# An attention kernel whose last block is rearranged: second half normalised without a cast in between, its guard on GpSimd, the last store issued by ScalarE, closing waits on five engines

## The chip, the cores and the metric

The kernel runs on one core of a Trainium2 chip. The metric is device microseconds of one execution, as the median of several runs; lower is better. One more execution is recorded by the hardware profiler, and its trace gives the rows that are quoted here. Engines: PE is TensorE's matmuls and PEld its weight loads, DVE is VectorE, ACT is ScalarE, POOL is GpSimd, SP is SyncE; a name with a q behind it (SPq, ACTq, POOLq) is that engine's sequencer, which issues DMAs, waits and branches.

## The reference: what is computed

Two attention blocks on different inputs, their outputs side by side. S is 2048 positions, D 640 channels, 32 heads of 20 channels, all in bf16.

```python
qkv = (x @ wqkv).reshape(B, S, 3, H, Dh)          # both blocks
# A: softmax attention
scores = jnp.einsum("bhqd,bhkd->bhqk", q, k) * (Dh ** -0.5)
o = jnp.einsum("bhqk,bhkd->bhqd", softmax(scores), v)
a = o.reshape(B, S, D) @ wo
# B: linear attention
phi = lambda t: jnp.where(t > 0, t + 1, jnp.exp(t)) + 1e-6
kv = jnp.einsum("bhsd,bhse->bhde", phi(k), v); z = phi(k).sum(s)
o = (phi(q) @ kv) / (phi(q) @ z + 1e-6)
b = o.reshape(B, S, D) @ wo
return jnp.concatenate([a, b], axis=-1)
```

## The kernel before

Block A does nearly all the work. It is cut into 32 blocks: 4 chunks of 512 queries times 8 groups of 4 heads. For each block and each of 16 tiles of 128 keys, PE makes the scores of the four heads, and their exponential is taken: by ScalarE for most tiles (L1976), by VectorE and GpSimd for 4 or 5 tiles of each block (L1829 turns a score into an integer that is the bits of a bf16 power of two, L2047 adds constants to four of these at once with a 64-bit add on GpSimd). PE multiplies the result with V into one PSUM bank, with a column of ones in V so that the softmax's denominator comes along. Block B's steps fill the gaps.

At the end of a block, `norm` (L2053 and on) has VectorE transpose the bank, take the reciprocal of the denominators into f_Rt, multiply into f_T and transpose back into f_OTn, from where a DMA spreads it for the output projection. The last block does this in two halves of 256 queries (`half`, L2073), so that the projection of the first half can start early. That last projection is cut into seven pieces (`CLOSE`, L795): for each the planner opens a PSUM bank with the groups that are done, and `step_close` adds the last group, has the engine that CLOSE names cast the piece into f_PT (L1420), and when the five columns of 128 of a tile are complete, issues its store (L1409). Tile 0 and 1 belong to the first half, tile 2 and 3 to the second.

The kernel skips the usual subtraction of the row maximum, so a guard (`check`, L2155) looks at the reciprocals: two compares against 1e-30 and 1e28 into a scratch (printed as f_xT), a reduction with minimum into f_sm (L2168), one small matmul over the partitions and two small steps (L2180, L2182) that leave a flag of 0 or 1. The reciprocals of the earlier blocks are looked at once before the end; those left over are looked at behind the last half. At the very end every engine reads the flag (L2429) and branches (L2432): to the end, or to a general version that computes block A anew (not run for these inputs). The end is `finish` (L198): waits for each of 24 DMA semaphores, two to an instruction.

The order of instructions on each engine is made when the program is built: a planner (`run`, `try_pe`, `try_q`) plays through estimated times, and each engine's queue gives, of the steps that are ready, the one of lowest `prio`. What it decides is then fixed; on the chip each engine runs its list in order, and waits at semaphores.

At the start, GpSimd loads the library that holds the 64-bit add (L1097) and makes the identity matrix f_id (MEMSET L1099, AFFINE_SELECT L1100). PE first runs 16 matmuls on zeros (f_zt), then transposes the first four tiles of x with f_id (L1126), then makes the first projections of Q and K.

Of the kernel before, what the change touches and what calls it, by code (L numbers as in the profile page):

```python
# [42 lines left out]
class _Sched:  # L43
# [152 lines left out]
                    eng.h.wait_ge(self.sems[key], 16 * cnt)  # L196

    def finish(self):  # L198
        sp = self.eng["sp"]
        for key, cnt, _ in self.dma_slots:  # L200
            if cnt > 0:
                sp.h.wait_ge(self.sems[key], 16 * cnt)


def _split_units(nunits):
# [519 lines left out]


class _Op:
    __slots__ = ("eng", "fn", "reads", "writes", "occ", "lat", "prio", "seq", "after", "ok", "dma")

    def __init__(self, eng, fn, reads, writes, occ, lat, prio, seq, after=None, ok=None):  # L730
        self.eng = eng
        self.fn = fn
        self.reads = reads
        self.writes = writes
        self.occ = occ
        self.lat = lat
        self.prio = prio
        self.seq = seq
        self.after = after
        self.ok = ok  # L740
        self.dma = eng == "sp"


def _c_dve(n):
    return 1.042 * n + 68
# [35 lines left out]
class _Fast:  # L781
# [10 lines left out]
    QO = "xVKVQKVQKV"  # L792
    HINT = {mybir.EngineType.PE: 3, mybir.EngineType.Activation: 9, mybir.EngineType.DVE: 6,
            mybir.EngineType.Pool: 13, mybir.EngineType.SP: 15}
    CLOSE = (("dve", 0, ((0, 0, 512),)), ("act", 0, ((1, 0, 512),)), ("act", 0, ((0, 512, 640), (1, 512, 640))),  # L795
             ("dve", 1, ((2, 0, 320),)), ("act", 1, ((2, 320, 640),)),
             ("dve", 1, ((3, 0, 320),)), ("act", 1, ((3, 320, 640),)))
    NS = 7
# [189 lines left out]
    def emit(self, op):  # L988
        e = op.eng
        t = max(self.free[e], self.est(e, op.reads, op.writes))  # L990
        if op.dma and e == "pool":
            s = max(t + 1450.0, self.dfree)
            self.dfree = s + 2900.0
            op.lat += s - t - 1450.0 + (2000.0 if t < 32000.0 else 0.0)
        if op.dma:
            self.sch.dma(e, op.fn, reads=op.reads, writes=op.writes)
        else:
            self.sch.op(e, op.fn, reads=op.reads, writes=op.writes)
        self.free[e] = t + op.occ
        self.mark(e, op.reads, op.writes, t + op.lat)  # L1000
        if op.after is not None:
            op.after()
# [390 lines left out]
    def step_close(self, qc, p):  # L1393
        eng, half, parts = self.CLOSE[p]
        flat = self.PT[:].rearrange("p t n -> p (t n)")
        w = parts[0][2] - parts[0][1]
        sl = [flat[:, 1024 * t + c0:1024 * t + c1] for t, c0, c1 in parts]
        if len(parts) == 2:
            t, c0, c1 = parts[0]
            sl = flat[:, 1024 * t:1024 * (t + 2)].rearrange("p (t n) -> p t n", n=1024)[:, :, c0:c1]  # L1400
        else:
            sl = sl[0]

        def fin(b):
            self.abank.append(b)
            for t, c0, c1 in parts:
                self.clw[t] = self.clw.get(t, 0) + c1 - c0
                if self.clw[t] == D_MODEL:
                    self.push("sp", lambda e, t=t: e.dma_start(  # L1409
                        self.out[512 * qc + 128 * t:512 * qc + 128 * (t + 1), 0:D_MODEL],  # L1410
                        flat[:, 1024 * t:1024 * t + D_MODEL]),
                        tuple(("cl", q) for q, c in enumerate(self.CLOSE) if any(y[0] == t for y in c[2])),
                        (("out", "a", t),), 500, prio=-1, lat=3000)

        def post(b):
            src = self.ps[:, b, 0:w * len(parts)]
            if len(parts) == 2:
                src = src.rearrange("p (t n) -> p t n", n=w)
            n = w * len(parts)
            self.push(eng, (lambda e: e.copy(sl, src)) if eng == "act" else (lambda e: e.tensor_copy(sl, src)),  # L1420
                      (("ps", b),), (("cl", p),), _c_act(n) if eng == "act" else _c_dve(n), prio=0,
                      after=lambda: fin(b))
        st = _Step(lambda b: self.out_mms(b, qc, parts, (6,)), post, needs=(("open", p),), key=("out", p))
        st.bank = p
        return st
# [624 lines left out]
    def norm(self, n):  # L2050
# [22 lines left out]
        def half(h):  # L2073
            c = slice(256 * h, 256 * (h + 1))
            bl = slice(8 * h, 8 * (h + 1))
            res = (("OTn", o), ("OTn", o, h))
            nxt = (lambda: (self.close(0), half(1))) if h == 0 else (lambda: self.normed(n))
            self.push("dve", lambda e: e.transpose(ps[:, b, c], ps[:, b, c]), (), (("ps", b),), 330, prio=-1,
                      ok=lambda: ("OTn", n - 1) in self.done, after=lambda: self.push(
                          "dve", lambda e: e.reciprocal(R[:, bl], Tv[:, bl, 0]), (("ps", b),), (("Rt", n),), 120,  # L2080
                          prio=-1, after=lambda: self.push(
                              "dve", lambda e: e.tensor_tensor(
                                  T2v[:, bl, 1:21], Tv[:, bl, 1:21],
                                  R[:, bl].unsqueeze(2).broadcast_to([128, 8, D_HEAD]), op=ALU.mult),
                              (("ps", b), ("Rt", n)), ("T2",), _c_dve(160), prio=-1,
                              after=lambda: (freed() if h else None, self.push(
                                  "dve", lambda e: e.transpose(self.OTn[:, o, c], self.T2[:, c]), ("T2",), res,
                                  330, prio=-1, after=nxt,
                                  ok=lambda: self.opv[n] is None or ("OTs", self.opv[n]) in self.done)))))
        if n == self.NN - 1:  # L2090
            half(0)
            return
        self.push("dve", lambda e: e.transpose(ps[:, b, :], ps[:, b, :]), (), (("ps", b),), 630, prio=-1,  # L2093
# [13 lines left out]
    def normed(self, n):  # L2107
# [39 lines left out]
                    ("dd", "bfin"))))  # L2147
        if g == N_GRP - 1 and last:
            self.close(1)
            assert self.chk >= 0  # L2150
            self.check(self.chk + 1, n)
        if last and self.chk < 0 and ("Q", self.NN - 1) in self.done and not self.qa:
            self.sch.barrier(("dve", "pool"), tuple(x for k in range(self.NQC) for x in self.xt(k)))
            self.chk = n
# [2 lines left out]
    def check(self, n0, n1):  # L2157
# [3 lines left out]
        w = b - a  # L2161
        G = self.gt[:, k, 0:2 * w]
        rd = tuple(("Rt", n) for n in range(n0, n1 + 1))
        self.push("dve", lambda e: e.tensor_scalar(G[:, 0:w], R, 1e-30, None, op0=ALU.is_ge), rd, (("G", k),),
                  _c_dve(w), prio=3, after=lambda: self.push(
                      "dve", lambda e: e.tensor_scalar(G[:, w:2 * w], R, 1e28, None, op0=ALU.is_le),
                      rd + (("G", k),), (("G", k),), _c_dve(w), prio=3, after=lambda: self.push(
                          "dve", lambda e: e.tensor_reduce(self.gm[:, k:k + 1], G, axis=AX.X, op=ALU.min),  # L2168
                          (("G", k),), (("gm", k),), _c_dve(2 * w), prio=3,
                          after=lambda: (self.done.add(("gm", k)), self.prio.append(self.step_flag()) if k == 1 else None))))  # L2170

    def step_flag(self):
# [331 lines left out]
```

## Time and profile before

| what | value |
|---|---|
| median of 3 runs | 718.08 us (718.06 to 720.66) |
| the profiled execution | 718.23 us |
| its span, first to last instruction | 716.5 us |
| TensorE clock granted | 0.998 |
| busy: PE, ACT, DVE, POOL | 98%, 97%, 86%, 46% of the span |

The span is what the rows of the profile count in; 1.73 us lie around it. Times in a row are microseconds from the start of the span. In a timeline a row gives start, length, engine, line, operation and tiles, then how many instructions it groups, and in brackets the idle time before it with what ended that. A row of one line's instructions gives their durations as least, median and largest in ns, and the starts of the first and the last.

### The profile page before, as it was taken

Reading aid. Unit: us, or ns where it says so; the run is one execution under the profiler, and the core shown is the slowest. Engines: PE = TensorE matmul, PEld = TensorE weight load, DVE = VectorE, ACT = ScalarE, POOL = GpSimd, SP = SyncE. Lnnn points to the kernel's source line nnn. Section 1 sums busy time; section 2 is a strip of 40 time slices with the busy share of each in tenths; the row PEclk is TensorE's granted clock in tenths of the full one; section 3 lists DMA queues with packets and bytes.
Section 4 is the critical chain, followed back from the end, with each engine's and each line's share of the span. In section 5 each row is a group of like instructions: output and inputs, shape, how many; then the busy total and the mean of one; then the engine's idle time right before and its main releaser. Section 6 shows DMA issues by size and latency. Waiting matters only on the chain.

```text
span 716.5 us, 25681 instructions
## 1 busy us (share of the span) xinstructions
PE 701.2 (98%) x11235; PEld 243.1 (34%) x11235; DVE 614.0 (86%) x1107; ACT 691.9 (97%) x772; POOL 331.1 (46%) x331
## 2 busy tenths in 40 slices
PE   8999999999899999999999999899999999999998
PEld 5433333333223332332432343233332333333323
DVE  6989878888888899989899987899898888998993
ACT  4789999999999999999999999999999999999996
POOL 7643344544445454445534355423454444443552
PEclk9999999999999999999999999999999999999999
DMA  9401010102330011010000112201021100010001
GB/s 264 108 19 36 16 25 14 38 11 74 84 62 11 17 49 43 3 37 21 13 12 9 38 37 86 47 21 28 15 49 31 48 18 8 27 28 7 20 17 48
DMA packets 46554, 27.59 MB, mean 39 GB/s; under 512 B 30842, under 2 KB 45882, under 8 KB 46442
## 3 DMA queue, kind: packets, MB, share of 16 engines
q1 hardware_dynamic: 43818, 23.98, 13.7%
q10 hardware_dynamic: 2624, 1.97, 1.0%
q8 instruction: 88, 1.44, 0.8%
q14 instruction: 24, 0.20, 0.1%
HBM read 8.40 MB, written 5.24 MB: 19 GB/s over the span
## 4 chain that ended last, share of the span: by engine, by line
PE 57%; ACT 39%; DVE 3%; DMA 1%; issue 0%; SPq 0%; ACTq 0%; DVEq 0%
PE ps L166 56%; ACT f_PT L1976 37%; DVE f_Sr L1829 2%; ACT f_ar L1468 2%; DMA f_PT<-in_A_x_dram 1%; DVE ps L2093 0%; PE ps L1047 0%; DVE f_ar L1274 0%; DVE f_st L1027 0%; PE ps L1126 0%; DVE f_PT L1420 0%; DVE f_Qr L1295 0%; DVE f_KT L1295 0%; DVE f_sq L1258 0%; SPq L1067 0%
## 5 line engine op out<-in xcount | busy, mean ns | idle before, releaser
L1976 ACT ACTIVATE f_PT<-ps 128x1024 bf16<-128x1024 f32 x724 | 675.2, 1088 | 13.0 <-PE ps L166 12.2
L2047 POOL INT64_ADD f_Sr<-f_Sr x300 | 307.7, 1041 | 366.2 <-PE ps L166 320.4
L1829 DVE TENSOR_SCALAR f_Sr<-ps 128x512 int16<-128x512 f32 x600 | 401.4, 683 | 65.4 <-PE ps L166 60.1
L166 PE MATMUL ps<-f_Qr,f_KT 32*128 32x512 bf16 x2048 | 285.0, 385 | 8.7 <-ACT f_PT L1976 7.2
L166 PEld LDWEIGHTS ps<-f_Qr,f_KT 32*128 32x128 bf16 x2048 | 71.6, 91 | 256.1 <-ACT f_PT L1976 228.6
L166 PE MATMUL ps<-f_ar 128*32 128x512 bf16 (+6 forms) x3024 | 144.6, 295 | 0.8 <-DVE f_Sr L1829 0.4
L166 PE MATMUL ps<-f_PT,f_V 128*21 128x512 bf16 x1448 | 135.1, 383 | 0.1
L166 PE MATMUL ps<-f_Sr,f_V 128*21 128x512 bf16 x1200 | 108.4, 384 | 0.0
L166 PEld LDWEIGHTS ps<-f_ar 128*32 128x32 bf16 x3024 | 55.8, 96 | 59.2 <-issue 37.2
L166 PE MATMUL ps<-f_Sr,f_Vp 128*21 128x512 bf16 x600 | 57.6, 382 | 0.0
L166 PEld LDWEIGHTS ps<-f_PT,f_V 128*21 128x21 bf16 x1448 | 34.3, 90 | 46.9 <-issue 38.7
L166 PEld LDWEIGHTS ps<-f_Sr,f_V 128*21 128x21 bf16 x1200 | 26.9, 90 | 34.1 <-issue 25.2
L166 PE MATMUL ps<-f_ar,f_xT 128*32 128x160 bf16 x1280 | 33.9, 234 | 0.5 <-DVE f_Sr L1829 0.2
L166 PE MATMUL ps<-f_wo,f_OTd 128*32 128x512 bf16 (+5 forms) x608 | 30.4, 302 | 0.0
L166 PE MATMUL ps<-f_xT,f_ar 128*32 128x512 bf16 x400 | 29.7, 382 | 0.0
L1470 DVE TENSOR_SCALAR f_ar<-f_ar 128x512 bf16<-128x512 bf16 x40 | 23.7, 592 | 4.0 <-ACT f_ar L1468 2.7
L1472 DVE SCALAR_TENSOR_TENSOR f_ar<-ps,f_ar 128x512 bf16<-128x512 f32 x40 | 26.9, 673 | 0.2
L166 PEld LDWEIGHTS ps<-f_ar,f_xT 128*32 128x32 bf16 x1280 | 22.4, 96 | 13.6 <-issue 8.6
L1468 ACT ACTIVATE f_ar<-ps 128x512 bf16<-128x512 f32 x40 | 26.6, 664 | 0.0
L1027 DVE CAST f_st<-ps 128x512 bf16<-128x512 f32 x35 | 23.9, 682 | 2.9 <-PE ps L166 2.6
L166 PE MATMUL ps<-f_xT,f_wq 128*32 128x512 bf16 x320 | 24.1, 383 | 0.0
L2093 DVE STREAM_TRANSPOSE ps<-ps 128x512 f32<-128x512 f32 x31 | 22.5, 725 | 1.8 <-PE ps L166 1.7
(76 smaller groups left out, 279.2 us busy)
## 6 DMA issues: line engine op xcount, KB each, us to landing
out_dram<-f_st SPq DMA_DIRECT2D x35, 128.0 KB
f_ar<-in_B_wqkv_dram SPq DMA_DIRECT2D x15, 160.0 KB
f_OTd<-f_OTn SPq DMA_DIRECT2D x105, 20.0 KB
f_Qr<-f_sq SPq DMA_DIRECT2D x88, 20.0 KB
f_KT<-f_ar SPq DMA_DIRECT2D x22, 80.0 KB
f_ar<-in_A_wqkv_dram SPq DMA_DIRECT2D x1, 800.0 KB
f_ar<-in_A_wqkv_dram ACTq DMA_DIRECT2D x1, 800.0 KB
f_wq<-in_A_wqkv_dram ACTq DMA_DIRECT2D x1, 800.0 KB
```

The source lines that it names most:

```text
L166: lambda e: e.matmul(out, lhsT, rhs, start=start, stop=stop, tile_position=tp, skip_group_check=sgc),
L1027: (lambda e: e.tensor_copy(sl, ps[:, b, 0:w])), (("ps", b),), (res,),
L1468: self.push("act", lambda e: e.activation(r1, src, AF.Exp), (("ps", b),), (rk,), _c_act(n), prio=0, ok=ok, after=lambda: self.push("dve", ...
L1470: "dve", lambda e: e.tensor_scalar(r1, r1, 1.0, 1e-6, op0=ALU.min, op1=ALU.add), (rk,), (rk,),
L1472: "dve", lambda e: e.scalar_tensor_tensor(dst, src, 0.0, r1, op0=ALU.max, op1=ALU.add),
L1829: post = lambda: self.push("dve", lambda e: e.tensor_scalar(self.Sr[:, s, i, :], self.ps[:, b, :], 0.0, 32639.0 - self.PH[-1], op0=ALU.max ...
L1976: return _Op("act", lambda e: e.activation(self.PT[:, s0:s0 + n, :], ps[:, b0:b0 + n, :], AF.Exp, scale=math.log(2.0) / 128.0, bias=self.l ...
L2047: self.q["pool"].append(_Op("pool", lambda e: e.int64_add(v, v, inc), res, res, self.C64, self.C64 + 150, 0, self.seq, after))
L2093: self.push("dve", lambda e: e.transpose(ps[:, b, :], ps[:, b, :]), (), (("ps", b),), 630, prio=-1, ok=lambda: n == 0 or ("OTn", n - 1) in ...
```

## The change

Only the last block and the end are touched.

- `finish` deals the 24 waits in turn to PE, ScalarE, GpSimd, VectorE and SyncE.
- In `CLOSE`, the cast of tile 0's first 512 columns goes from VectorE to ScalarE, and that of the last 128 columns of tiles 0 and 1 from ScalarE to VectorE.
- In `half`, transpose, reciprocal and multiply are one item for the planner (`parts`), so that no other step of VectorE comes between them.
- The second `check` is pushed when the last half is multiplied, its two compares run on GpSimd, and its reduction has the prio -0.5 in place of 3.
- The store of tile 3 is issued by ScalarE.

```diff
     def finish(self):
-        sp = self.eng["sp"]
+        engs = [self.eng[n] for n in ("pe", "act", "pool", "dve", "sp") if n in self.eng]
+        k = 0
         for key, cnt, _ in self.dma_slots:
             if cnt > 0:
-                sp.h.wait_ge(self.sems[key], 16 * cnt)
+                engs[k % len(engs)].h.wait_ge(self.sems[key], 16 * cnt)
+                k += 1
...
-    CLOSE = (("dve", 0, ((0, 0, 512),)), ("act", 0, ((1, 0, 512),)), ("act", 0, ((0, 512, 640), (1, 512, 640))),
+    CLOSE = (("act", 0, ((0, 0, 512),)), ("act", 0, ((1, 0, 512),)), ("dve", 0, ((0, 512, 640), (1, 512, 640))),
              ("dve", 1, ((2, 0, 320),)), ("act", 1, ((2, 320, 640),)),
              ("dve", 1, ((3, 0, 320),)), ("act", 1, ((3, 320, 640),)))
...
-            self.sch.op(e, op.fn, reads=op.reads, writes=op.writes)
+            for fn, rd, wr in op.parts or ((op.fn, op.reads, op.writes),):
+                self.sch.op(e, fn, reads=rd, writes=wr)
...
                 if self.clw[t] == D_MODEL:
-                    self.push("sp", lambda e, t=t: e.dma_start(
+                    q = "act" if t == 3 else "sp"
+                    self.push(q, lambda e, t=t: e.dma_start(
                         self.out[512 * qc + 128 * t:512 * qc + 128 * (t + 1), 0:D_MODEL],
...
+            self.push("dve", None, (), (("ps", b), ("Rt", n), "T2"), 980, prio=-1,
+                      ok=lambda: ("OTn", n - 1) in self.done,
+                      after=lambda: ((freed(), self.check(self.chk + 1, n)) if h else None, self.push(
+                          "dve", lambda e: e.transpose(self.OTn[:, o, c], self.T2[:, c]), ("T2",), res, 440, prio=-1,
+                          after=nxt, ok=lambda: self.opv[n] is None or ("OTs", self.opv[n]) in self.done)))
+            self.q["dve"][-1].parts = (
+                (lambda e: e.transpose(ps[:, b, c], ps[:, b, c]), (), (("ps", b),)),
+                (lambda e: e.reciprocal(R[:, bl], Tv[:, bl, 0]), (("ps", b),), (("Rt", n),)),
+                (lambda e: e.tensor_tensor(T2v[:, bl, 1:21], Tv[:, bl, 1:21],
+                                           R[:, bl].unsqueeze(2).broadcast_to([128, 8, D_HEAD]), op=ALU.mult),
+                 (("ps", b), ("Rt", n)), ("T2",)))
...
             self.close(1)
-            assert self.chk >= 0
-            self.check(self.chk + 1, n)
...
-        self.push("dve", lambda e: e.tensor_scalar(G[:, 0:w], R, 1e-30, None, op0=ALU.is_ge), rd, (("G", k),),
-                  _c_dve(w), prio=3, after=lambda: self.push(
-                      "dve", lambda e: e.tensor_scalar(G[:, w:2 * w], R, 1e28, None, op0=ALU.is_le),
-                      rd + (("G", k),), (("G", k),), _c_dve(w), prio=3, after=lambda: self.push(
+        eng, p, cost = ("pool", 0, 240) if k else ("dve", 3, _c_dve(w))
+        self.push(eng, lambda e: e.tensor_scalar(G[:, 0:w], R, 1e-30, None, op0=ALU.is_ge), rd, (("G", k),),
+                  cost, prio=p, after=lambda: self.push(
+                      eng, lambda e: e.tensor_scalar(G[:, w:2 * w], R, 1e28, None, op0=ALU.is_le),
+                      rd + (("G", k),), (("G", k),), cost, prio=p, after=lambda: self.push(
                           "dve", lambda e: e.tensor_reduce(self.gm[:, k:k + 1], G, axis=AX.X, op=ALU.min),
-                          (("G", k),), (("gm", k),), _c_dve(2 * w), prio=3,
+                          (("G", k),), (("gm", k),), _c_dve(2 * w), prio=-0.5 if k else 3,
```

What the planner makes of this on VectorE, from the reciprocal of the second half to the branch. ps is PSUM, f_Rt the reciprocals, f_T the normalised half, f_PT the casts for the stores, f_sm the guard's minimum; a row's brackets name the engines whose semaphores it waits for. Before:

```order
L2080 RECIPROCAL f_Rt<-ps 128x8 [waits f_sem_dve]
L1420 CAST f_PT<-ps 128x512 [waits f_sem_pe]
L2082 TENSOR_TENSOR f_T<-ps,f_Rt 128x8x20 [waits f_sem_dve]
L2087 STREAM_TRANSPOSE f_OTn<-f_T 128x256 [waits f_sem_dve]
L2164 TENSOR_SCALAR f_xT<-f_Rt 128x64
L2166 TENSOR_SCALAR f_xT<-f_Rt 128x64 [waits f_sem_dve]
L1420 CAST f_PT<-ps 128x320 [waits f_sem_pe] x2
L2168 TENSOR_REDUCE f_sm<-f_xT 128x1 [waits f_sem_dve]
L2180 TENSOR_REDUCE f_g<-ps 1x1 [waits f_sem_pe]
```

And now:

```order
L2091 RECIPROCAL f_Rt<-ps 128x8 [waits f_sem_dve]
L2092 TENSOR_TENSOR f_T<-ps,f_Rt 128x8x20 [waits f_sem_dve]
L1426 CAST f_PT<-ps 128x2x128 [waits f_sem_pe]
L2087 STREAM_TRANSPOSE f_OTn<-f_T 128x256 [waits f_sem_dve]
L2173 TENSOR_REDUCE f_sm<-f_xT 128x1 [waits f_sem_pool]
L1426 CAST f_PT<-ps 128x320 [waits f_sem_pe] x2
L2185 TENSOR_REDUCE f_g<-ps 1x1 [waits f_sem_pe]
```

The 512-wide cast is gone from between reciprocal and multiply, a cast of 2x128 stands behind the multiply, the two compares have left, and the reduction stands ahead of the two last casts, with a wait for GpSimd.

GpSimd, from its 64-bit adds on (printed ISA f_Sr). What stands behind the branch (COMPARE_AND_BRANCH) belongs to the general version. An ISA row without tiles is an instruction that names a library of GpSimd; one more stands at the program's start, for L1097. Before:

```order
L2054 BRANCH_PREFETCH_HINT
L2047 ISA f_Sr<-f_Sr 128x1024 x114
L2429 TENSOR_LOAD f_flag
L2432 COMPARE_AND_BRANCH
L303 MEMSET a_wkp 128x5120
L304 MEMSET a_wqp 128x5120
L314 ISA
L314 IOTA a_ident_i 128x128
```

And now:

```order
L2060 BRANCH_PREFETCH_HINT
L2053 ISA f_Sr<-f_Sr 128x1024 x114
L2169 ISA
L2169 TENSOR_SCALAR f_xT<-f_Rt 128x64
L2171 TENSOR_SCALAR f_xT<-f_Rt 128x64
L2434 TENSOR_LOAD f_flag
L2437 COMPARE_AND_BRANCH
L305 MEMSET a_wkp 128x5120
L306 MEMSET a_wqp 128x5120
L316 IOTA a_ident_i 128x128
```

The two compares have come, and the bare ISA row, which stood in the general version ahead of IOTA, now stands ahead of the first compare, in the part that is always run. The code does not name it; the build puts it in, ahead of an instruction that the add's library does not hold.

ScalarE, from its exponentials on. Before:

```order
L1976 ACTIVATE f_PT<-ps 128x1024 [waits f_sem_pe] x60
L1420 CAST f_PT<-ps 128x512 [waits f_sem_pe]
L1420 CAST f_PT<-ps 128x2x128 [waits f_sem_pe]
L1420 CAST f_PT<-ps 128x320 [waits f_sem_pe] x2
L2429 TENSOR_LOAD f_flag [waits f_sem_dve]
```

And now:

```order
L1982 ACTIVATE f_PT<-ps 128x1024 [waits f_sem_pe] x60
L1426 CAST f_PT<-ps 128x512 [waits f_sem_pe] x2
L1426 CAST f_PT<-ps 128x320 [waits f_sem_pe] x2
L1414 DMA out_dram<-f_PT 128x640 [waits f_sem_act,f_sem_dve]
L2434 TENSOR_LOAD f_flag [waits f_sem_dve]
```

The 2x128 cast has become a second 512-wide one, and the last store stands behind the casts and waits for VectorE's part of them.

More of the change, by code (lines that the diff above doesn't have):

```diff
@@ L727 @@
 class _Op:
-    __slots__ = ("eng", "fn", "reads", "writes", "occ", "lat", "prio", "seq", "after", "ok", "dma")
+    __slots__ = ("eng", "fn", "reads", "writes", "occ", "lat", "prio", "seq", "after", "ok", "dma", "parts")
     def __init__(self, eng, fn, reads, writes, occ, lat, prio, seq, after=None, ok=None):
@@ L741, in __init__ @@
         self.dma = eng == "sp"
+        self.parts = ()
 def _c_dve(n):
@@ L1413, in fin @@
                         (("out", "a", t),), 500, prio=-1, lat=3000)
+                    self.q[q][-1].dma = True
         def post(b):
@@ L2077, in half @@
             nxt = (lambda: (self.close(0), half(1))) if h == 0 else (lambda: self.normed(n))
[L2078 to L2089, printed above, removed]
+            self.push("dve", None, (), (("ps", b), ("Rt", n), "T2"), 980, prio=-1,
[9 more added lines that the diff above has]
+                 (("ps", b), ("Rt", n)), ("T2",)))
         if n == self.NN - 1:
+            assert self.chk >= 0
             half(0)
```

## The prediction

> **What bounds the kernel now.** The page comes first: its first part gives each engine's share of the span.
>
> ```profile
> span 716.5 us, 25681 instructions
> PE 701.2 (98%) x11235; PEld 243.1 (34%) x11235; DVE 614.0 (86%) x1107; ACT 691.9 (97%) x772; POOL 331.1 (46%) x331
> ```
>
> TensorE is busy for 98% and ScalarE for 97%. So whatever holds TensorE up at the start moves the whole program to the right, and whatever holds up the last stores is added at the end; between the two there is nothing to win, and the change touches only the end. The busy times by stretch say how early that begins (columns: stretch, its length, then busy time and count of PE, PEld, DVE, ACT, POOL, then clock, DMA share, GB/s):
>
> ```profile
> 0.00:5.00 5.00, 3.94 (x22) 2.75 (x23) 0.71 (x7) 1.49 (x2) 1.20 (x8) 1.00 0.60 161
> 5.00:10.00 5.00, 4.77 (x65) 3.33 (x63) 2.73 (x7) 1.39 (x2) 3.67 (x5) 1.00 1.11 338
> 10.00:15.00 5.00, 4.41 (x98) 2.48 (x94) 4.85 (x10) 2.93 (x4) 5.00 (x5) 1.00 1.26 276
> 15.00:20.00 5.00, 4.99 (x154) 2.74 (x142) 4.59 (x9) 3.93 (x5) 5.00 (x4) 1.00 1.15 263
> ```
>
> From 15 us on PE has no hole (4.99 of 5.00). A delay in the first 10 us that every matmul inherits is therefore paid in full.
>
> Then the last 10 us, from the timelines of VectorE, ScalarE, GpSimd and SyncE (start, length, instruction, count):
>
> ```profile
> 706.59 1.05 POOL L2047 INT64_ADD f_Sr<-f_Sr  x1 [2.48 <-PE ps L166]
> ...
> 710.76 0.21 DVE L2080 RECIPROCAL f_Rt<-ps 128x8 f32<-128x8 f32 x1
> 710.98 0.69 DVE L1420 CAST f_PT<-ps 128x512 bf16<-128x512 f32 x1
> 711.59 0.32 DVE L2082 TENSOR_TENSOR f_T<-ps,f_Rt 128x160 bf16<-128x160 f32 x1
> 711.94 0.45 DVE L2087 STREAM_TRANSPOSE f_OTn<-f_T 128x256 bf16<-128x256 bf16 x1
> 712.31 0.15 DVE L2164 TENSOR_SCALAR f_xT<-f_Rt 128x64 f32<-128x64 f32 x1
> 712.49 0.20 DVE L2166 TENSOR_SCALAR f_xT<-f_Rt 128x64 f32<-128x64 f32 x1
> 712.81 0.89 DVE L1420 CAST f_PT<-ps 128x320 bf16<-128x320 f32 x2
> 713.62 0.28 DVE L2168 TENSOR_REDUCE f_sm<-f_xT 128x1 f32<-128x128 f32 x1
> 714.17 0.15 DVE L2180 TENSOR_REDUCE f_g<-ps 1x1 f32<-1x2 f32 x1 [0.28 <-PE ps L166]
> 714.35 0.14 DVE L2182 TENSOR_SCALAR f_flag<-f_g 1x1 int32<-1x1 f32 x1
> ...
> 711.19 0.86 ACT L1420 CAST f_PT<-ps 128x512 bf16<-128x512 f32 x2 [2.88 <-PE ps L166]
> 712.95 0.75 ACT L1420 CAST f_PT<-ps 128x320 bf16<-128x320 f32 x2 [0.89 <-PE ps L166]
> ...
> 712.13 2.12 SPq L1409 DMA_DIRECT2D out_dram<-f_PT  x4
> ```
>
> VectorE works without a hole from the reciprocal of the second half to the reduction of the guard at 713.90, then the flag follows at 714.49. The lines that use the flag and the closing waits:
>
> ```profile
> L2429 SPq TENSOR_LOAD <-f_flag x1: 738/738/738, 714.5 to 714.5; - x1
> ...
> L202 SPq EVENT_SEMAPHORE  x12: 28/28/28, 715.5 to 716.2; - x12
> ```
>
> Every engine reads the flag (0.74 us) and branches; then SyncE alone runs 12 wait instructions, 0.06 us apart (0.76 us by their starts and the end of the last, 715.52 to 716.28), none of them held up. DMA traffic of the window 712.0 to 716.5 (40 slices of 0.1125 us):
>
> ```profile
> DMA  0000000029998999930069997999810000000022
> ```
>
> The last store's traffic ends in the thirtieth slice, by 715.4. Its issue ended at 712.13 + 2.12 = 714.25, so it needs 1.15 us more.
>
> **The change part by part.** The kernel's own time is the profiled execution's: 718.23 us, 1.73 more than its span, and 0.15 over the median 718.08; sums are made on 718.23. By "what a measurement of this kernel can tell from no change" I take 0.5%, 3.6 us.
>
> *Second half without a cast in between.* The 0.69 us CAST that stood between reciprocal and multiply goes to ScalarE, the multiply follows at 711.0 and a CAST of 2x128 comes behind it; by the 320-wide one (0.89 for two) I price it at 0.4. The transpose to f_OTn then ends at about 712.07 instead of 712.39: 0.3 us won ahead of the last matmuls and casts. ScalarE's extra 512-wide cast lies in its hole of 2.88 us before 711.19 or behind it, ended by 711.9: free.
>
> *Guard on GpSimd.* VectorE loses 0.15 + 0.20 us of compares, which in before lie while PE makes the last matmuls (CAST waits until 712.81), so nothing is won there. But the reduction moves ahead of the two last CASTs of VectorE and waits for GpSimd. Behind that wait stand the two CASTs, behind them the store that ScalarE now issues, and the flag.
>
> *Last store on ScalarE.* Its issue no longer queues behind the third on SyncE; it follows the last CAST, as now. Between 0 and 0.4 us (one issue, a quarter of the 2.12 us of four, less its wait) won; I take 0, since the fourth issue began only as the CAST had ended.
>
> *Multiply, reciprocal and transpose as one planned item* fixes their order and adds no instruction; PE's last small matmul now also waits for a bank that ScalarE frees, by 713.70 as now, before the reduction is there: nothing.
>
> *Closing waits over five engines.* 24 waits become 4 or 5 per engine: 2 or 3 of the 12 instructions instead of 12, 0.06 us each: 0.5 us less, down to the landing of the last store, which lies about where the waits begin now. The cover is that landing; without a later landing the end is 715.6 to 715.7.
>
> Were this all, the end would come 0.9 us earlier: 717.3.
>
> *The library switch.* The rows of the instruction order show one more instruction than the diff: ahead of GpSimd's first compare stands a bare ISA row. Such a row stands once more on the executed path, at L1097, where the code loads the GpSimd library that holds the 64-bit add. What the profile makes of that one:
>
> ```profile
> L1097 POOLq MODIFY_POOL_CONFIG  x2: 11/11/11, 0.9 to 0.9; - x2
> ...
> 0.96 0.20 POOL L1099 MEMSET f_id<- 128x128 bf16 x1 [0.45 <-POOLq L2489]
> 1.24 0.29 POOL L1100 TENSOR_SCALAR_AFFINE_SELECT f_id<-f_id 128x128 bf16<-128x128 bf16 x1
> ```
>
> Two instructions of 11 ns, and GpSimd is at work 0.03 us later. That is one bound: a switch costs nothing. But in before the execution that went ahead left the same library in place (its last GpSimd work is the 64-bit add), so I read these rows as a switch to what is there already, which says nothing on a real one. In the changed kernel each execution ends with the other library, so it would pay twice: for that one at the end, and for the add's library at its start. No row shows code being loaded. The nearest are transfers from HBM, cold, in the same first microseconds:
>
> ```profile
> 0.80 1.10 ACTq L1071 DMA_DIRECT2D f_ar<-in_A_wqkv_dram  x2
> ...
> 4.97 0.38 POOL L1143 COPY f_wqp<-f_ar 128x240 bf16<-128x240 bf16 x1 [2.97 <-DMA f_ar<-in_A_wqkv_dram]
> 6.62 0.39 POOL L1143 COPY f_ar<-f_ar 128x240 bf16<-128x240 bf16 x1 [1.27 <-DMA f_ar<-in_A_wqkv_dram]
> ```
>
> The first 160 KB were usable 4.2 us after their issue, the second 5.3 us after theirs (issued halfway, at about 1.3). A real switch is one such transfer (4.2) at least, and two of them one after the other (9.5) at most, since it is two instructions; I take the middle, 6.8 us.
>
> At the start the identity matrix f_id is made behind the switch, and PE's transposes wait for it:
>
> ```profile
> 4.45 1.27 PE L1126 MATMUL ps<-f_id,f_PT 128*128 128x128 bf16 x10
> 5.95 1.24 PE L1126 MATMUL ps<-f_id,f_PT 128*128 128x128 bf16 x10 [0.23 <-DMA f_PT<-in_A_x_dram]
> 6.99 1.07 PE L166 MATMUL ps<-f_zt 128*128 128x256 bf16 x8
> 8.02 1.26 PE L166 MATMUL ps<-f_xT,f_wqp 128*32 128x512 bf16 x20
> ```
>
> Now f_id is ready at 1.53, 0.6 behind the switch, and waits 2.9 us for the first x tiles: that is the cover. With 6.8 us it is ready at 0.93 + 6.8 + 0.6 = 8.33; the first ten transposes run 8.4 to 9.66, the second ten start there instead of at 5.95: 3.7 us late. The projections and all else behind follow. So the start costs 3.7 (1.1 with 4.2 us, 6.4 with 9.5).
>
> At the end the ISA row waits for nothing, so it starts behind the last 64-bit add, at 707.64. The compares need the reciprocal of 710.97: 3.3 us of cover. With 6.8 us GpSimd is ready at 714.44. Two compares: by the AFFINE_SELECT row 0.29 each with 0.08 between, as between that row and the MEMSET before it (bounds 0.15, VectorE's own, and 0.39, the COPY): 715.10. Reduction 715.15 to 715.43, CASTs (0.89) to 716.34, ScalarE's issue (0.38) to 716.77, traffic 1.15 to 717.9, then 0.3 for a last wait and the closing (716.28 to 716.5 now): 718.25 against 716.5, that is 1.75 late. The flag comes out level: its two small steps (0.32) behind the CASTs and 1.03 from its end to the first closing wait, as now, give 717.7, and three waits 717.9. (With 4.2 us the compares end at 712.5, the reduction fits ahead of the CASTs almost free, and the end comes 0.8 early; with 9.5 it is 4.4 late.)
>
> Sum: 718.23 + 3.7 + 1.75 = 723.7. Ends: 718.23 + 1.1 - 0.8 = 718.5 and 718.23 + 6.4 + 4.4 = 729.0.
>
> [...]
>
> **The rivals.**
>
> *The switch is free.* For it: the only switch in this trace is (11 ns). Against: that one changed nothing. Then the start stands as it is and the end comes 0.9 earlier: 717.3, no change that can be told. It decides for any load under 2.9 us at the start (the cover of f_id) and 3.3 at the end. Chance 0.20.
>
> *The load begins only with the first call.* The instruction itself takes 11 ns and returns, so the load may wait until a compare asks for it, at 711.0, and the 3.3 us of cover are gone. The end is then 3.4 later than forecast (717.8 instead of 714.44): 727.1. At the start nothing differs, as the AFFINE_SELECT calls at once. Chance 0.15. [...]
>
> *One end only.* If something between two executions puts the add's library back, the start stays and only the end pays: 720.0. If the end's load is covered and the start pays: 718.23 + 3.7 - 0.9 = 721.0. Nothing in one trace tells. Chance 0.12.
>
> *More than that.* PE idles from the end of its first warm-up matmuls at 4.65 to 8.4. Those ran slowly at first:
>
> ```profile
> 1.06 3.59 PE L166 MATMUL ps<-f_zt 128*128 128x256 bf16 x16 [1.06 <-DVE f_sm L1104]
> ```
>
> 16 in 3.59 us is 0.22 each, against 0.13 for the eight of 6.99. If PE falls back to that pace for as long again, 1.5 us come on top, 725.2 for the forecast; with a load of over 9.5 us the time goes past 728. Chance of over 728: 0.08.
>
> **How the numbers follow.** The forecast itself, both ends paid and the load begun by the instruction, has 0.45; its own range is 721.9 to 726.0. Below 721.7 (0.5% over the median) lie the free switch, the single ends and a tenth of the forecast: 0.20 + 0.12 + 0.04, of which 0.02 I leave for a gain of over 3.6 us that no row supports. Slower by over 0.5%: 0.41 + 0.15 + 0.08 and a little of the single ends, 0.65. The range must reach the free switch, since without it 0.28 would be left out: 717.2 to 727.6, which leaves out the longest loads alone.
>
> **What would show each step.** In the changed profile: MODIFY_POOL_CONFIG a second time, at the guard's line, after 707; a hole on GpSimd between 0.9 and the AFFINE_SELECT, and PE's first transposes near 8.4 instead of 4.45, with the waits naming f_id; near the end VectorE's reduction waiting for GpSimd, with the two 320-wide CASTs behind it, and the last store's issue on ScalarE's queue behind those. Closing waits of 2 or 3 on each of five engines. The forecast is wrong if the AFFINE_SELECT still starts near 1.2 (only the end pays, or nothing), or if the reduction finds the compares done by 712.1 (a free switch). If the compares start 6 to 7 us behind the reciprocal and not behind the last add, the load begins with the call.

## The result, and the profile after

| | before | after |
|---|---|---|
| median of 6 runs, us | 718.07 (717.08 to 720.66) | 726.00 (724.97 to 726.44) |
| ratio | | 1.0109, 95% interval 1.0092 to 1.0126 |
| the profiled execution, us | 718.23 | 724.97 |
| its span, us | 716.5 | 723.2 |

The kernel became slower by 7.9 us by the medians (the ratio, here and below, is estimated from all runs and is not the quotient of the medians). The page of after shows the same work on each engine as before; only the span has grown:

```profile
span 723.2 us, 25685 instructions
PE 700.5 (97%) x11235; PEld 243.0 (34%) x11235; DVE 613.1 (85%) x1105; ACT 691.7 (96%) x772; POOL 332.1 (46%) x333
```

So the time has gone into holes, and the place to look is where GpSimd changes its library. The rows of the two lines concerned, the start of the program (L1101) and the guard (L2169), with least, median and largest duration in ns and the starts of first and last:

```profile
L1101 POOLq MODIFY_POOL_CONFIG  x2: 11/11/11, 1.0 to 1.1; - x2
...
L2169 POOLq MODIFY_POOL_CONFIG  x2: 11/11/11, 711.7 to 711.7; - x2
```

The switch is there twice, and its own rows still say 11 ns. What it costs stands in the brackets of the next rows of GpSimd. Timelines of after, GpSimd and TensorE, in the first microseconds:

```profile
8.89 0.20 POOL L1103 MEMSET f_id<- 128x128 bf16 x1 [8.39 <-issue]
9.16 0.29 POOL L1104 TENSOR_SCALAR_AFFINE_SELECT f_id<-f_id 128x128 bf16<-128x128 bf16 x1
...
1.05 3.60 PE L166 MATMUL ps<-f_zt 128*128 128x256 bf16 x16 [1.05 <-DVE f_sm L1108]
9.61 2.29 PE L1130 MATMUL ps<-f_id,f_PT 128*128 128x128 bf16 x20 [4.96 <-POOL f_id L1104]
11.69 1.63 PE L166 MATMUL ps<-f_zt 128*128 128x256 bf16 x8
13.25 1.26 PE L166 MATMUL ps<-f_xT,f_wqp 128*32 128x512 bf16 x20
```

GpSimd has nothing to wait for but the switch ("issue" names no engine and no transfer) and still begins the identity at 8.89, 7.8 us behind the switch at 1.09, where before began it at 0.96. TensorE stands 4.96 us, and the bracket names f_id. The first projections start at 13.25 instead of 8.02. By stretch (columns as in the prediction) the second five microseconds, in which before had PE busy for 4.77, are almost empty:

```profile
5.00:10.00 5.00, 0.40 (x5) 0.43 (x6) 0.47 (x4) 0.00 (x0) 1.03 (x4) 1.00 1.11 338
10.00:15.00 5.00, 5.00 (x61) 3.56 (x63) 2.82 (x9) 1.38 (x2) 4.94 (x6) 1.00 0.90 166
```

Then the end, from the timelines of GpSimd, VectorE and ScalarE in after:

```profile
710.65 1.04 POOL L2053 INT64_ADD f_Sr<-f_Sr  x1 [2.48 <-PE ps L166]
718.87 0.41 POOL L2169 TENSOR_SCALAR f_xT<-f_Rt 128x64 f32<-128x64 f32 x1 [7.18 <-issue]
719.36 0.38 POOL L2171 TENSOR_SCALAR f_xT<-f_Rt 128x64 f32<-128x64 f32 x1
...
714.81 0.21 DVE L2091 RECIPROCAL f_Rt<-ps 128x8 f32<-128x8 f32 x1
715.70 0.44 DVE L2087 STREAM_TRANSPOSE f_OTn<-f_T 128x256 bf16<-128x256 bf16 x1
719.78 0.29 DVE L2173 TENSOR_REDUCE f_sm<-f_xT 128x1 f32<-128x128 f32 x1 [3.64 <-POOL f_xT L2171]
719.98 0.88 DVE L1426 CAST f_PT<-ps 128x320 bf16<-128x320 f32 x2
720.95 0.14 DVE L2187 TENSOR_SCALAR f_flag<-f_g 1x1 int32<-1x1 f32 x1
...
717.00 0.76 ACT L1426 CAST f_PT<-ps 128x320 bf16<-128x320 f32 x2 [0.89 <-PE ps L166]
720.89 0.38 ACTq L1414 DMA_DIRECT2D out_dram<-f_PT  x1
```

The reciprocals that the compares read are ready at 715.02; the compares start at 718.87, 7.18 us behind the last 64-bit add and not behind the reciprocal. VectorE's reduction waits 3.64 us for them, its two casts queue behind that, and the store behind the casts. Lastly the closing waits of after (`finish`), now on five engines:

```profile
L203 ACTq EVENT_SEMAPHORE  x3: 17/38/38, 722.3 to 722.5; - x3
L203 PEldq EVENT_SEMAPHORE  x3: 51/51/51, 722.4 to 722.7; - x3
L203 DVEq EVENT_SEMAPHORE  x3: 21/49/50, 722.5 to 722.6; - x3
L203 SPq EVENT_SEMAPHORE  x2: 28/28/28, 722.1 to 722.1; - x2
L203 POOLq EVENT_SEMAPHORE  x2: 43/43/43, 722.8 to 722.9; - x2
```

Two terms make the loss. At the start, the first exponential of ScalarE begins at 17.31 instead of 12.07 (rows of ScalarE, before, then after): 5.24 us.

```profile
12.07 5.73 ACT L1976 ACTIVATE f_PT<-ps 128x1024 bf16<-128x1024 f32 x6 [4.16 <-PE ps L166]
```

```profile
17.31 2.86 ACT L1982 ACTIVATE f_PT<-ps 128x1024 bf16<-128x1024 f32 x3 [4.69 <-PE ps L166]
```

At the end, from the second half's reciprocal to the end of the span, before takes 716.5 - 710.76 = 5.74 and after 723.2 - 714.81 = 8.39: 2.65 us. Together 7.89, close to the difference of the medians (7.93). That it is so close is partly chance, since the start's term differs from one execution to the next: with the same switch at their start, E2 and E7 below begin their first exponential at 18.47 and 18.51. The two profiled executions differ by 6.74 only. The reciprocal stands 714.81 - 710.76 = 4.05 later, not 5.24, because the profiled execution of before had a stretch of lower clock that after's had not. After's exponentials are 5.22 us later up to the one at 453.95 in before (459.18 in after), and 4.06 later from the one at 460.74 on (464.80). PE's clock there is the third number from the end; before, then after:

```profile
450.00:460.00 10.00, 8.58 (x97) 2.45 (x93) 8.29 (x18) 9.17 (x12) 5.09 (x5) 0.83 0.20 47
```

```profile
450.00:460.00 10.00, 8.58 (x109) 2.46 (x105) 7.88 (x16) 10.00 (x13) 0.55 (x1) 1.00 0.21 48
```

### The profile page after: what moved, and what is told of

Its sections match the earlier page's. It is cut to its first block, busy times and chain, and to the rows that moved or that the text cites. A ratio compares the mean times of both kernels' runs of the same rounds, so it can differ in the third digit from the quotient of the medians.

```text
span 723.2 us, 25685 instructions
## 1 busy us (share of the span) xinstructions
PE 700.5 (97%) x11235; PEld 243.0 (34%) x11235; DVE 613.1 (85%) x1105; ACT 691.7 (96%) x772; POOL 332.1 (46%) x333
## 3 DMA queue, kind: packets, MB, share of 16 engines
HBM read 8.40 MB, written 5.24 MB: 19 GB/s over the span
## 4 chain that ended last, share of the span: by engine, by line
PE 55%; ACT 39%; DVE 4%; issue 2%; POOL 0%; POOLq 0%; ACTq 0%; DVEq 0%
PE ps L166 54%; ACT f_PT L1982 37%; DVE f_Sr L1835 2%; ACT f_ar L1474 2%; DVE ps L2099 0%; PE ps L1051 0%; PE ps L1130 0%; DVE f_ar L1278 0%; DVE f_st L1031 0%; DVE f_PT L1426 0%; DVE ps L2090 0%; DVE f_Qr L1299 0%; DVE f_OTn L2087 0%; DVE f_KT L1299 0%; DVE f_sq L1262 0%
```

## The experiments

The theory: a real switch of GpSimd's library is paid twice, at the end for the compares' library and at the start of the next execution for the add's. The rivals: the loss comes from the other edits of the end (the guard's order, the store, the waits); or the load starts only when an instruction calls for the new library; or only one end pays. The kernel before, timed beside them, had a median of 717.12 for E1 to E4 and of 718.14 for E5 to E7.

**E1: all of the change but the switch.** The compares go back to VectorE, the reduction to its old place.

```diff
-        eng, p, cost = ("pool", 0, 240) if k else ("dve", 3, _c_dve(w))
+        eng, p, cost = "dve", 3, _c_dve(w)
...
-                          (("G", k),), (("gm", k),), _c_dve(2 * w), prio=-0.5 if k else 3,
+                          (("G", k),), (("gm", k),), _c_dve(2 * w), prio=3,
```

> The changed kernel with the guard's two compares back on VectorE (reduction behind the last casts again); all else of the change stays, and no library is switched. Theory (the two library loads are the whole loss): start as in before, end 0.9 us earlier by the prediction's sum, 717.2 us against 718.07. Rival one (the rearranged end itself, the last store on ScalarE or the closing waits on five engines cost too): of the 2.65 us by which the end is longer, measured from the second half's reciprocal, a part stays, 718.5 to 720.7. Rival two (the hole at the start comes from something else in the changed program than the guard's library): 723 or more.

Measured: 716.93 us, ratio 0.9994 (0.9978 to 1.001). The whole loss is gone, and what is left of the change is worth nothing that can be measured. E1's timelines of GpSimd, VectorE, TensorE and ScalarE:

```profile
1.25 0.29 POOL L1104 TENSOR_SCALAR_AFFINE_SELECT f_id<-f_id 128x128 bf16<-128x128 bf16 x1
...
710.29 0.21 DVE L2091 RECIPROCAL f_Rt<-ps 128x8 f32<-128x8 f32 x1
711.18 0.43 DVE L2087 STREAM_TRANSPOSE f_OTn<-f_T 128x256 bf16<-128x256 bf16 x1
...
711.30 0.72 PE L166 MATMUL ps<-f_wo,f_OTd 128*32 128x320 bf16 x16
711.84 0.85 PE L166 MATMUL ps<-f_wo,f_OTn 128*32 128x320 bf16 x20
...
712.47 0.75 ACT L1426 CAST f_PT<-ps 128x320 bf16<-128x320 f32 x2 [0.89 <-PE ps L166]
```

f_OTn is ready 1.32 us behind the reciprocal, where before needed 1.63. But the last matmuls that read it start 1.55 behind the reciprocal in both (before: 712.31 against 710.76, in this row of its TensorE):

```profile
712.31 0.85 PE L166 MATMUL ps<-f_wo,f_OTn 128*32 128x320 bf16 x20
```

TensorE has the f_OTd matmuls in hand until then without a hole, so the earlier operand finds a busy engine, and ScalarE's last casts follow 2.18 us behind the reciprocal, as in before (712.95 against 710.76). The span ends 716.0 - 710.29 = 5.71 behind the reciprocal, against 5.74: the 0.9 us that the prediction gave to the rest of the change are not there.

**E2: the switch alone.** Before, with a load of the other library ahead of the last block's halves, which nothing uses.

```diff
         if n == self.NN - 1:
+            self.nc.gpsimd.load_library(library_config.all_libraries[0])
             half(0)
```

> The kernel before with one instruction more: after the last 64-bit add GpSimd is told to load the other library, and nothing uses it. Theory (an execution finds the library that the one ahead of it left): the start pays the load of 7.8 us and is 5.2 later, the end pays nothing, since the load is over (707.7 + 7.1 = 714.8) before GpSimd has to read the flag's branch: 723.3 us. Rival (a load costs only where an instruction calls for the library, so this one never happens, or the start does not depend on what is left behind): 718.1 us.

Measured: 723.07 us, ratio 1.0075 (1.0051 to 1.0099). E2's timelines of GpSimd and TensorE, and its busy times of one stretch:

```profile
8.88 0.19 POOL L1099 MEMSET f_id<- 128x128 bf16 x1 [8.38 <-issue]
...
9.59 2.29 PE L1126 MATMUL ps<-f_id,f_PT 128*128 128x128 bf16 x20 [4.94 <-POOL f_id L1100]
...
10.00:15.00 5.00, 5.00 (x42) 3.31 (x44) 2.38 (x8) 1.38 (x2) 4.94 (x6) 0.50 0.89 171
```

The hole at the start is that of after, though nothing ever called the library loaded at the end: what the previous execution leaves behind decides the start. The end, 721.7 - 715.96 = 5.74, is that of before. In this execution the start's shift is 6.40 us instead of 5.24; the granted clock reads 0.50 here between 10 and 15 us, and 1.00 in after.

**E3: switching back.** After, with the add's library loaded again behind the second compare.

```diff
-                      rd + (("G", k),), (("G", k),), cost, prio=p, after=lambda: self.push(
+                      rd + (("G", k),), (("G", k),), cost, prio=p, after=lambda: (self.nc.gpsimd.load_library(library_config.all_libraries[1]) if k else None, self.push(
```

> The changed kernel, and behind the guard's two compares GpSimd is told to load the add's library again, so that the next execution finds it. Theory: the start is free (AFFINE_SELECT near 1.2 us), the end has its 2.65 us as in the changed kernel. If GpSimd reads the flag and closes while the load runs: 720.7 us. If the close waits for the load (7.1 us from the compares' end, about 3.5 us past the present close): 724 us. Rival (the start does not depend on what is left behind): 726 us or more, with the start's hole as in the changed kernel.

Measured: 720.03 us, ratio 1.0039 (1.0024 to 1.0055). E3's timeline of GpSimd:

```profile
1.24 0.29 POOL L1104 TENSOR_SCALAR_AFFINE_SELECT f_id<-f_id 128x128 bf16<-128x128 bf16 x1
...
715.26 0.41 POOL L2169 TENSOR_SCALAR f_xT<-f_Rt 128x64 f32<-128x64 f32 x1 [7.66 <-issue]
```

The start is whole again (first exponential at 12.06, before 12.07), and only the end pays: 719.6 - 710.73 = 8.87 from reciprocal to end, against 5.74 in before and 8.39 in after. The second load, behind the compares, which end at 716.13, holds nothing up that shows: the flag ends at 717.48, GpSimd is at its closing waits at 719.2, and the span ends at 719.6. E2 and E3 together part the loss into a start and an end, and refute the rival that only one of them pays. By the medians they add 5.95 and 2.91 us, 0.9 more together than the change lost; in the profiled executions E2's start is 1.16 later than after's, and E3's load at the end is 0.48 longer.

**E4: the identity ahead of the switch.** After, with the start's load moved behind f_id. It was meant to give back the start.

```diff
-        self.nc.gpsimd.load_library(library_config.all_libraries[1])
         idn = self.ident
...
                                                  channel_multiplier=1), writes=("ident",))
+        self.nc.gpsimd.load_library(library_config.all_libraries[1])
```

> The changed kernel with the identity matrix made ahead of the switch to the add's library: the library left by the execution before holds AFFINE_SELECT too (the build sets a switch to it in front, which should be free, as it is there already). Theory: PE's transposes start at 4.4 us as in before; the load then holds GpSimd from about 1.5 to 9.3, so that its COPY of the weights (in before at 6.6) comes at 9.4 to 10.1 and the projections start near 10.2 instead of 8.0 or 13.25: 3.0 us won, 723.0 us. Rival (the start is late for another reason than the wait for f_id): 725 to 726 us. If a switch to the library that is there is paid too, the start is 7 us later still: 733 us.

Measured: 725.61 us, ratio 1.0116 (1.0091 to 1.014): nothing given back. E4's row of a switch that the build puts in front of AFFINE_SELECT, its timelines of GpSimd and TensorE, and one stretch:

```profile
L1103 POOLq MODIFY_POOL_CONFIG  x2: 11/11/11, 1.2 to 1.2; - x2
...
1.28 0.29 POOL L1103 TENSOR_SCALAR_AFFINE_SELECT f_id<-f_id 128x128 bf16<-128x128 bf16 x1 [0.29 <-POOL f_id L1102]
10.84 0.51 POOL L1107 MEMSET f_T<- 128x512 bf16 x1 [9.26 <-issue]
...
11.83 1.60 PE L166 MATMUL ps<-f_xT,f_wqp 128*32 128x512 bf16 x20 [4.35 <-POOL f_wqp L1147]
13.17 2.38 PE L166 MATMUL ps<-f_xT,f_ar 128*32 128x512 bf16 x20
...
10.00:15.00 5.00, 3.17 (x40) 1.47 (x40) 1.50 (x2) 0.00 (x0) 4.11 (x6) 0.76 1.16 324
```

f_id was ready in time and the transposes ran at 4.43, as in before. But the load took 9.26 us, and GpSimd's copy of the weights (f_wqp), which before made at 4.97, stood behind it. TensorE waited 4.35 us for that instead of 4.96 for f_id, and then made 20 projections in 2.38 us that take 1.27 in before. The expectation had the copies behind the load, and the projections at 10.2; it took the load 1.5 us too short, and left out TensorE's slower pace behind its waiting. So the first exponential starts at 16.90, only 0.4 ahead of after's 17.31 instead of 3.0. The time falls where the rival had it, 725 to 726, and in part for the rival's reason: f_id is not the only thing that TensorE waits for. What makes the start late is that GpSimd stands still; f_id is the first of its products that is missed, and f_wqp the next.

**E5: and the weight copies on ScalarE.** E4, with the two copies of f_wqp and f_ar moved off GpSimd.

```diff
-            sch.op("pool", lambda e, dst=dst, k=k: e.tensor_copy(
+            sch.op("act", lambda e, dst=dst, k=k: e.copy(
```

> The identity-first kernel of the run before, and the two copies of weight rows that GpSimd made behind the load are made by ScalarE, which idles there. In that run PE lay idle 4.4 us for the first of them, and its next 40 matmuls ran at a lower granted clock. Theory (each load costs what no longer hides it, nothing else): projections start near 8.2 us as in before, PE keeps its clock, the load of some 9 us goes on beside them; what is left is the end's 2.65 us, +2.9 us over the kernel before (about 720). Rival: GpSimd's other start work (the fills of V, Q and K, in before over at 23.5, now some 4 us later) holds the first 64-bit add and through it PE: +4 to +7 us.

Measured: 723.82 us, ratio 1.0095 (1.0074 to 1.0116), with single runs from 721.39 to 727.16. E5's timelines of GpSimd, TensorE and ScalarE:

```profile
10.50 0.52 POOL L1107 MEMSET f_T<- 128x512 bf16 x1 [8.92 <-issue]
...
28.57 0.40 PE L166 MATMUL ps<-f_Sr,f_V 128*21 128x512 bf16 x4 [1.77 <-POOL f_Sr L2053]
...
33.36 2.85 ACT L1982 ACTIVATE f_PT<-ps 128x1024 bf16<-128x1024 f32 x3 [1.05 <-PE ps L166]
```

The first exponential now starts at 12.22 instead of 12.07, so the load's wait for f_id and f_wqp is covered. The 8.92 us of load do not vanish, though: GpSimd's later work of the start is late, and TensorE waits 1.77 us for the first 64-bit add. The exponential of the last row starts at 31.39 in before, so the program is now 1.97 us late. With the end, 719.7 - 711.58 = 8.12 from reciprocal to end instead of 5.74, that makes 1.97 + 2.38 = 4.35 us. It lies in the rival's range, and most of the 1.97 comes by its mechanism. The profiled run, 721.39, is only 3.2 over before's 718.23, near the theory's 2.9, but that is luck: the stretch of lower clock behind 450 us cost before's profiled execution 1.2 us, and this one has none. So the theory, that the end's 2.65 us are all that is left, was wrong. The median is 5.7 over 718.14, also in the rival's range, but not by that mechanism alone. The other five runs are slower than the profiled one, and they go with TensorE's mean granted clock: 721.39 at 0.998, 723.45 to 724.04 at 0.995 and 0.996, 726.39 and 727.16 at 0.991 (time by clock is 719.9 to 720.6 in all six). Where in the program those runs lost their clock, no trace shows; that stays open.

**E6: the closing waits alone.** Before, with the new `finish`.

```diff
-        sp = self.eng["sp"]
+        engs = [self.eng[n] for n in ("pe", "act", "pool", "dve", "sp") if n in self.eng]
+        k = 0
...
-                sp.h.wait_ge(self.sems[key], 16 * cnt)
+                engs[k % len(engs)].h.wait_ge(self.sems[key], 16 * cnt)
+                k += 1
```

> The kernel before with the closing waits dealt to five engines, nothing else. The prediction's step: 0.5 us less between the flag's end and the end of the span (2.0 us in before, 1.5 then). Rival, as the changed kernel's rows suggest (SyncE's two waits end at 722.2, GpSimd's start at 722.8): the other engines come out of the branch up to 0.7 us after SyncE, and the sum is 1.9 to 2.1 us as now. In the time neither can be told from 718.07 by more than 0.1%; the rows decide.

Measured: 717.10 us, ratio 0.9999 (0.9983 to 1.0014). E6's row of the flag, and the rows of its closing waits:

```profile
712.68 0.14 DVE L2184 TENSOR_SCALAR f_flag<-f_g 1x1 int32<-1x1 f32 x1
...
L203 ACTq EVENT_SEMAPHORE  x3: 17/38/38, 714.1 to 714.2; - x3
L203 PEldq EVENT_SEMAPHORE  x3: 51/51/51, 714.2 to 714.4; - x3
...
L203 SPq EVENT_SEMAPHORE  x2: 28/28/28, 713.8 to 713.9; - x2
```

SyncE is done early, at 713.9, but TensorE only comes to its first wait at 714.2 and to its last at 714.4. From the end of the flag to the end of the span it is 714.8 - 712.82 = 2.0 us, as in before (716.5 - 714.49). The 0.5 us of the prediction are not won, as the rival had it.

**E7: the reduction last.** After, with the guard's reduction behind the two casts, so that the stores wait for no compare.

```diff
-                          (("G", k),), (("gm", k),), _c_dve(2 * w), prio=-0.5 if k else 3,
+                          (("G", k),), (("gm", k),), _c_dve(2 * w), prio=3, ok=lambda: not k or self.clw.get(3) == D_MODEL,
```

> The changed kernel with VectorE's reduction put behind its two last casts again; the compares stay on GpSimd, both loads stay. Theory (the end is late by the load and by what stands behind the reduction): the casts run as they would without a wait, the last two stores leave 3 us earlier, but the flag still waits for the compares: it comes 0.4 us earlier (from the last 64-bit add's start 9.9 instead of 10.4 us), and the time stays 7.4 us over the kernel before. Rival (the casts and the store held behind the reduction are the end's loss): the end's 2.65 us go, 5.2 us over before are left.

Measured: 725.66 us, ratio 1.0104 (1.0086 to 1.0123): 7.5 us over the kernel before that was timed beside it, where the theory had 7.4. E7's timelines of GpSimd, VectorE and ScalarE:

```profile
720.37 0.41 POOL L2169 TENSOR_SCALAR f_xT<-f_Rt 128x64 f32<-128x64 f32 x1 [7.39 <-issue]
...
721.27 0.29 DVE L2173 TENSOR_REDUCE f_sm<-f_xT 128x1 f32<-128x128 f32 x1 [2.23 <-POOL f_xT L2171]
...
719.13 0.38 ACTq L1414 DMA_DIRECT2D out_dram<-f_PT  x1
```

The last store now leaves at 719.13, 3.0 us behind the reciprocal (716.11) instead of 6.1. But every engine still has to read the flag before it may end, and the flag needs the compares: 723.9 - 716.11 = 7.8 us from reciprocal to end. That is 0.6 less than after's 8.39, although this execution's load is 0.2 longer (7.39 against 7.18): the flag ends 0.93 behind the compares instead of 1.35, and the span 1.73 behind the flag instead of 2.11. So the order of the reduction was worth some 0.8 us of the end in these two executions. The 2.06 us over before's 5.74 that are left come with the load and the compares behind it, and the rival, that the end's loss goes, is refuted. (The start's load took 8.46 us in this execution, f_id's MEMSET beginning at 9.56, and its first exponential starts at 18.51.)

## Why the prediction was right, and where its terms were off

The forecast was 723.7 us, the time 726.00. The number alone does not speak for it: it lies at the upper edge of the forecast's own range (721.9 to 726.0), and the rival in which the load begins only with the first call, at 727.1, came nearer. The rows decide between them.

**The switch, and that it is paid twice:** right, and shown. E1 takes it away and the loss goes; E2 adds it alone and three quarters of the loss come. The 11 ns in the profile of before were a switch to what was already there: in E4 the build puts a switch ahead of the identity, to the library that the previous execution had left, and the AFFINE_SELECT still starts at 1.28, behind two rows of 11 ns.

**The price of the load, 6.8 us:** too low by 1.0 at the start (7.8) and by 0.4 at the end (7.2), inside the bounds of 4.2 and 9.5.

**The start, forecast 3.7, measured 5.24:** the chain was as written, f_id, then the transposes, then everything behind. The longer load makes 1.0 of the difference: the second ten transposes start at about 10.7 (half of 2.29 behind 9.61), not 9.66. The other 0.5 is TensorE's slow pace: the 8 matmuls on zeros take 1.63 us instead of 1.07. A slow pace behind the waiting stood among the rivals at 1.5 us. It came, and cost a third of that, since before made its transposes at the slow pace too (1.27 for the first ten, where E4's second ten took 0.73). No fall of the pace shows here: the matmuls ahead of the waiting were slow already (16 in 3.60 us), and TensorE had not yet come to the quick pace when it had to stand still. The matmuls on zeros behind the transposes quicken from 0.21 us apart to 0.11 at 12.9, 3.3 us behind the first transpose. Whether 4.96 us of waiting slow a TensorE that is at the quick pace, after can't show, as it was slow ahead of them.

**The end, forecast 1.75, measured 2.65:** the load adds 0.4; GpSimd's compares take 0.41 and 0.38 where 0.29 each was read off the AFFINE_SELECT (0.87 for the pair instead of 0.66); the step from the last cast to the end took 723.2 - 720.86 = 2.34 instead of the 1.91 of the sum; reduction and casts together were 0.1 shorter. The sum went by the last store's way. By the rows the end goes by the flag: it ends at 721.09, and 2.11 us lie behind it, in which GpSimd comes to its closing waits last, at 722.8. That is 0.7 behind SyncE, where in E6 it is 0.3; no row names the reason.

**Second half without a cast, 0.3 us won:** won on VectorE, and lost again at TensorE (E1). The prediction had the transpose "ahead of the last matmuls" and did not look whether those were free to start.

**Closing waits, 0.5 us won:** wrong (E6). The step counted instructions, 12 against 2 or 3, and left out when the engines come to them. In before SyncE does twelve between 715.52 and 716.28; spread out, ACT, PE, DVE and POOL are only there some 0.2 to 0.7 us behind SyncE (in after 722.3 to 722.8 against 722.1).

**The store on ScalarE and the guard's place, nothing won:** right as far as can be measured (E1); E7 prices the reduction's place ahead of the casts, with the load in front of it, at some 0.8; the rest of the end's loss it leaves, since the flag needs the compares itself.

**The rivals:** a free switch is refuted by after itself. A load that waits for the first call is refuted by the compares: 7.18 us behind the last add, 3.85 behind the reciprocal; with a load of 7.2 us begun at the reciprocal they would start at 722.2. One end only is refuted by E2 and E3.

## What to carry to other kernels

Before moving an instruction to GpSimd, see which library it comes from and which one is resident, and look in the order of the instructions for a switch that the code does not name; its own row said 11 ns here, and the cost was the idle time of the next GpSimd row (8.39 us at the start of after, 7.18 at its end). The switch near the end of this program was also one at its start (E2: f_id begun at 8.88 instead of 0.96). The load was covered only as long as nobody waited for anything that the engine made behind it: with f_id out of its way TensorE waited 4.35 us for the weight copies (E4), and with those moved too, 1.77 us for the first 64-bit add (E5). And an operand that came 0.31 us earlier was worth nothing, since the engine that takes it was busy until then (E1): read that engine's row ahead of the claim.

## What the runs showed of the hardware

- The switch held GpSimd's next instruction, a MEMSET (idle 8.39 us ahead of it in after, 9.26 in E4) as well as the first compare (7.18 in after). It overlapped waits for inputs: in after the compares start 7.18 us behind the last add and 3.85 behind their operand. It did not hold the reading of the flag: in E3 the compares end at 716.13 with a load behind them, the flag ends at 717.48, GpSimd is at its closing waits at 719.2 and the span ends at 719.6, and no load that was measured took under 6.84.
- Its length was 6.84 to 7.66 us at the end (E5 and E3) and 7.8 to 9.26 at the start (after and E4), where the DMA share of after reads 1.11 (5 to 10 us), against 0.03 and 0.19 at its end (710 to 715 and 715 to 720). Whether that traffic lengthens it is not shown; no run had a start without it.
- The library that one execution left was the one that the next found: f_id's MEMSET begins at 8.88 in E2, which loads the other library near its end, and at 0.96 in E3, which loads the add's again, as in before. A switch to the library that was there cost some 0.2 us at most (E4: 0.29 us idle ahead of AFFINE_SELECT, where before has 0.08).
- TensorE was slow at the start (16 matmuls on zeros in 3.60 us, 0.22 each), and slow for a while behind 4 to 5 us of idling in after, E2 and E4; in after and E2 it was slow ahead of the idling too. In E4 it had come to the quick pace ahead of 4.35 us of waiting (8 matmuls on zeros in 1.04 us), and behind it the first 20 projections took 1.60 us and the second 20 2.38, where before needs 1.26 and 1.27. How much it cost differed from run to run: 8 matmuls on zeros took 1.63 us in after and 1.91 in E2, where 1.07 is their time in before. The column of the granted clock showed it in E2 (0.50, 10 to 15 us) and in E4 (0.76) and not in after (1.00).
